# q and k of a fused attention and mixer kernel: turned on the tensor engine with PSUM evictions, or turned in 32x32 blocks on VectorE and placed by DMAs inside SBUF

## The chip, the cores and the metric

The kernel runs on one core of one Trainium2 chip. The metric is the device time of one execution in microseconds (us). Most executions of one kernel agree within about 1%, so differences of a few per cent are read from several executions. PE is the tensor engine (PEld its weight loads), DVE is VectorE, ACT is ScalarE, POOL is GpSimd, and SP is SyncE, which here only issues DMAs. "Clock" is the share of full speed that the chip granted to the tensor engine.

## The reference, cut to what matters

```python
# q, k, v: (8 batches, 8 heads, 576, 64), s: (8, 8, 576)
scores = scale * q @ k.T
cum = cumsum(max(s, 0))
scores = where(causal, -1e9, scores + min(-(cum[:, None] - cum[None, :]), 0))
attn = softmax(scores) @ v                      # per batch and head
x = attn.transpose(0, 2, 1, 3).reshape(8, 576, 512)
u = x + (x.T @ U @ V).T                         # mixing over the sequence, U: (576, 32)
out = u + max(u @ w_ch1, 0) @ w_ch2             # 512 -> 2048 -> 512
```

In these kernels both operands of the score product have head_dim (64) on the partitions and the sequence along the free axis: the page before lists line 223 as `68*128 68x128`, 64 rows of head_dim and 4 of the bias. In memory they lie the other way round, so q and k of all 64 heads are turned once.

## The kernel before

It works in bf16 and goes through head pairs, four pairs to a batch. `slots` hold a pair's score operands: 64 partitions of q and k, and 4 more partitions with the rows that carry the bias. q and k are loaded with sequence row 8p + t on partition p (72 partitions). Each head takes eight PE transposes into PSUM and two copies that evict it and put the columns in order:

```python
def transposes(n):                              # n: head pair
    b, hp = divmod(n, PB)
    slot = slots[n % NSLOT]
    if b > 0:
        nc.sync.dma_start(out=slot[D:KA, :, 0 : 2 * S], in_=rows_hbm[...])
    for hh in range(2):
        h = 2 * hp + hh
        tp = pwork().bitcast(BF16)[...]
        for c, src in enumerate((q_t[b], k_t[b])):
            for t2 in range(4):
                nc.tensor.transpose(            # line 202
                    tp[:, c, t2, :], src[:, h, ds(t2 * 128, 128)], identity[:TP, :TP]
                )
        dst = slot[0:D, hh, 0 : 2 * S].rearrange("p (c m t two) -> p c m t two", c=2, t=4, two=2)
        for par in range(2):
            copy = nc.scalar.copy if n < 2 else nc.vector.tensor_copy
            copy(dst[:, :, :, :, par], tp[par * D : par * D + D].rearrange("p c t m -> p c m t"))  # 208
        yield
```

The tensor engine is kept busy by "filling". The two large products of the previous batch (`chanmix`, 32 steps a batch) are generators, and every step of the attention work is followed by one step of filling:

```python
def run(gen):
    for _ in gen:
        step_fill()
# ... the opening: batch 0 without filling ...
for n in range(PB, NP + 1):
    b, hp = divmod(n, PB)
    if hp == 0 and b + 1 < B:
        alloc_qk(b + 1)
        load_qk(b + 1, 0, H)
        load_v(b + 1)
    if n + 1 < NP:
        run(transposes(n + 1))                  # one pair ahead
    if n < NP:
        run(scores(n))                          # PE, then exp on ACT, then masks on DVE
    if n > PB:
        run(values(n - 1))                      # PE, then normalization on DVE into x_sb
        if hp == 0:
            run(seqmix(b - 1))                  # its first matmul ("mixing") reads x_sb
            fill.append(chanmix(b - 1))
```

At the end of each batch the mixing matmul waits for the last normalization, and the filling of the next batch waits for the mixing.

The softmax here doesn't subtract the row's maximum and nothing guards it: scores larger than these inputs give would overflow.

## Time and profile before

| | before |
|---|---|
| time, median of 3 | 414.27 us (412.5, 414.27, and one execution of 1405.88 that is an outlier and is counted in the median) |
| PE busy | 391.6 us of the span of 412.1 |
| DVE, ACT busy | 228.5 us, 197.8 us |
| chain of waits | 91% PE |

The head of the page: busy us of each engine, its share of the span and its instructions, then busy tenths and granted clock in 40 equal slices.

```profile
span 412.1 us, 8636 instructions
...
PE 391.6 (95%) x3624; PEld 227.0 (55%) x3624; DVE 228.5 (55%) x452; ACT 197.8 (48%) x378; POOL 55.2 (13%) x73
...
PE   6188999989999999999999999999999999999996
...
PEclk9558999989999999999999999999999999999999
DMA  7999999992531945191619071100110001001002
```

PE is full except in the first slices, at the ninth (82 to 93 us), and at the very end. DVE has room. The DMA engines are full (nines in the DMA row) from the second through the ninth slice: weights and inputs are loading.

The chain of work that ended last, in order of time (start, duration, engine and line); first where filling and transposes alternate, then the hole at the end of batch 1.

```profile
47.59 0.26 PE pwork L202 x8
47.85 0.86 PE pwork L361 x4
48.71 0.26 PE pwork L202 x8
...
84.52 0.67 DVE slot_99 L208
85.19 0.37 DVE x_sb L286
...
85.59 0.80 DVE slot_99 L208
...
90.34 2.13 PE pwork L299 x5
```

One head's eight transposes put 0.26 us on the chain. The second part shows the hole: the filling has run out, and copies of line 208 and a slow mixing (L299: 2.13 us here, 1.08 us one batch later, at 133.98 us) stand in the chain. The granted clock from 88 to 92 us was 0.64.

The costs that the change removes, in the groups of instructions (line, engine, operation, output and input, shape, count; busy us and mean ns of one; idle time before and its releaser).

```profile
L208 DVE COPY slot_97<-pwork 64x576 bf16<-64x576 bf16 x24 | 19.2, 800 | 4.5 <-PE pwork L202 4.1
...
L202 PE MATMUL pwork<-identity,q_sd 72*128 72x72 bf16 x256 | 18.7, 198 | 1.4 <-ACT slot_96 L208 1.2
```

And one batch of the steady state, in the table by stretches (stretch, length, busy us and counts of PE, PEld, DVE, ACT, POOL; then clock, DMA share, GB/s):

```profile
134.00:177.00 43.00, 43.00 (x432) 25.38 (x431) 27.84 (x54) 22.51 (x44) 5.60 (x7) 1.00 0.49 69
```

PE is busy in all 43.00 us at full clock. This part of the kernel is bound by PE.

### The profile page before, as it was taken

To read this page: it belongs to the slowest core of one execution; us is meant where nothing else is said; L and a number is where in the kernel's file an instruction comes from. 1 tells how busy PE (TensorE), PEld (TensorE's weight loads), DVE (VectorE), ACT (ScalarE), POOL (GpSimd) and SP (SyncE) were. 2 spreads that over 40 slices of the span, in tenths; PEclk is the share of its full clock that TensorE was granted. 3 is DMA by queue.
4 is the path that set the end of the run, shared out by engine and by line. 5 is a ranking of instruction groups with operands and counts; after the bars stand their busy time and mean duration, and the time that the engine had idled before them with its cause. 6 is when DMAs were issued, how large, how long until landed. Compare 5 with 4: busy or idle time off the path is not lost.

```text
span 412.1 us, 8636 instructions
## 1 busy us (share of the span) xinstructions
PE 391.6 (95%) x3624; PEld 227.0 (55%) x3624; DVE 228.5 (55%) x452; ACT 197.8 (48%) x378; POOL 55.2 (13%) x73
## 2 busy tenths in 40 slices
PE   6188999989999999999999999999999999999996
PEld 2176556565556555555556556655565565444442
DVE  8267675686566756685666756575667545002011
ACT  3295384373743575337633663377336730530610
POOL 8721144040100310041004100000000000000000
PEclk9558999989999999999999999999999999999999
DMA  7999999992531945191619071100110001001002
GB/s 109 154 229 170 179 121 123 163 105 14 76 70 54 85 55 93 53 84 23 99 55 108 6 117 54 54 3 3 37 57 13 0 27 52 25 27 55 24 25 76
DMA packets 59301, 29.68 MB, mean 72 GB/s; under 512 B 42302, under 2 KB 53598, under 8 KB 59262
## 3 DMA queue, kind: packets, MB, share of 16 engines
q0 software_dynamic: 53360, 18.44, 52.4%
q1 hardware_dynamic: 5902, 10.69, 7.6%
q8 instruction: 28, 0.46, 0.5%
q14 instruction: 11, 0.09, 0.1%
HBM read 37.51 MB, written 9.95 MB: 115 GB/s over the span
## 4 chain that ended last, share of the span: by engine, by line
PE 91%; ACT 3%; DVE 2%; DMA 2%; issue 1%; ACTq 0%
PE pwork L361 30%; PE pwork L374 30%; PE pscore L223 11%; PE pwork L276 7%; PE pwork L202 4%; PE pwork L299 2%; PE pwork L385 2%; DMA slot_95<-hT 2%; PE pwork L320 2%; PE pscore L118 2%; PE pwork L312 1%; DVE uT L328 1%; DVE slot_99 L208 1%; ACT slot_96 L208 1%; ACT slot_95 L208 1%
## 5 line engine op out<-in xcount | busy, mean ns | idle before, releaser
L374 PE MATMUL pwork<-w_sb,hT 128*128 128x512 bf16 x576 | 143.8, 379 | 0.0
L361 PE MATMUL pwork<-uT,w_sb 128*128 128x512 bf16 x576 | 140.5, 379 | 0.4 <-DVE uT L328 0.4
L368 ACT ACTIVATE hT<-pwork 128x512 bf16<-128x512 f32 x144 | 87.4, 608 | 83.8 <-PE pwork L361 83.3
L361 PEld LDWEIGHTS <-w_sb 128*128 128x128 bf16 x576 | 51.1, 98 | 47.7 <-issue 0.9
L374 PEld LDWEIGHTS <-hT 128*128 128x128 bf16 x576 | 50.2, 98 | 42.7
L394 DVE COPY o_sb<-pwork 128x512 f32<-128x512 f32 x36 | 24.9, 692 | 70.8 <-PE pwork L385 70.8
L234 ACT ACTIVATE pT_89<-pscore 128x512 bf16<-128x512 f32 x32 | 19.2, 600 | 49.3 <-PE pscore L223 49.3
L234 ACT ACTIVATE pT_88<-pscore 128x512 bf16<-128x512 f32 x32 | 19.3, 604 | 42.4 <-PE pscore L223 42.4
L285 DVE RECIPROCAL rec<-pwork 128x5 f32<-128x5 f32 x64 | 12.2, 194 | 49.1 <-PE pwork L276 48.9
L286 DVE TENSOR_TENSOR x_sb<-pwork,rec 128x320 bf16<-128x320 f32 x64 | 31.0, 490 | 1.9
L235 DVE TENSOR_TENSOR pT_88<-pT_88,keep 128x512 bf16<-128x512 bf16 x32 | 13.1, 413 | 22.9 <-ACT pT_88 L234 22.9
L223 PE MATMUL pscore<-slot_95 68*128 68x128 bf16 (+4 forms) x126 | 15.6, 255 | 10.2 <-DMA slot_95<-hT 10.2
L276 PEld LDWEIGHTS <-pT_88 128*128 128x128 bf16 x480 | 20.1, 100 | 6.7 <-issue 0.2
L276 PEld LDWEIGHTS <-pT_89 128*128 128x128 bf16 x480 | 19.8, 100 | 7.1 <-issue 0.2
L243 ACT ACTIVATE pT_88<-pscore 128x512 bf16<-128x512 f32 x32 | 19.6, 612 | 7.5 <-PE pscore L223 6.2
L328 DVE CAST uT<-pwork 128x512 bf16<-128x512 f32 x32 | 20.1, 683 | 5.2 <-PE pwork L320 5.2
L202 PEld LDWEIGHTS <-q_sd 72*128 72x128 bf16 x256 | 16.1, 99 | 12.2 <-issue 1.6
L243 ACT ACTIVATE pT_89<-pscore 128x512 bf16<-128x512 f32 x32 | 19.3, 602 | 6.7 <-PE pscore L223 6.6
L208 DVE COPY slot_97<-pwork 64x576 bf16<-64x576 bf16 x24 | 19.2, 800 | 4.5 <-PE pwork L202 4.1
L208 DVE COPY slot_99<-pwork 64x576 bf16<-64x576 bf16 x24 | 19.2, 799 | 3.8 <-PE pwork L202 3.4
L208 DVE COPY slot_96<-pwork 64x576 bf16<-64x576 bf16 x24 | 19.2, 800 | 2.3 <-PE pwork L202 2.0
L202 PE MATMUL pwork<-identity,q_sd 72*128 72x72 bf16 x256 | 18.7, 198 | 1.4 <-ACT slot_96 L208 1.2
(91 smaller groups left out, 454.9 us busy)
## 6 DMA issues: line engine op xcount, KB each, us to landing
out_dram<-o_sb SPq DMA_DIRECT2D x36, 256.0 KB
w_sb<-in_moe_w_ch_dram POOLq DMA_DIRECT2D x2, 2048.0 KB, 25.1
q_sd<-in_q_dram POOLq DMA_DIRECT2D x7, 576.0 KB, 8.1
k_sd<-in_k_dram POOLq DMA_DIRECT2D x7, 576.0 KB, 11.2
v_slot_121<-in_v_dram POOLq DMA_DIRECT2D x12, 128.0 KB, 7.4
v_slot_124<-in_v_dram POOLq DMA_DIRECT2D x12, 128.0 KB, 5.3
v_slot_127<-in_v_dram POOLq DMA_DIRECT2D x8, 128.0 KB, 10.8
rows_hbm<-hT SPq DMA_DIRECT2D x1, 504.0 KB
```

What stands on the lines that cost most here:

```text
L202: nc.tensor.transpose(tp[:, c, t2, :], src[:, h, ds(t2 * 128, 128)], identity[:TP, :TP])
L208: copy(dst[:, :, :, :, par], tp[par * D : par * D + D].rearrange("p c t m -> p c m t"),)
L223: nc.tensor.matmul(dst, lhsT=kT[:, ds(j * 128, 128)], rhs=qT[:, lo:hi], start=True, stop=True,)
L234: nc.scalar.activation(pT[:, hh, 0:512], diag, EXP, scale=scale)
L243: nc.scalar.activation(pT[:, hh, 512:1024], far, EXP, scale=scale)
L276: nc.tensor.matmul(po[:, i, :], lhsT=pT[:, hh, ds(place(j, i), 128)], rhs=vt[:, j, h, :], start=(j == 0), stop=(j == i), skip_group_check= ...
L286: nc.vector.tensor_tensor(x_sb[:, :, ds(h * D, D)], po[:, :, 0:D], rec.to_broadcast([128, 5, D]), op=ALU.mult,)
L328: nc.vector.tensor_copy(uT[:, dt, ds(b * S, 512)], ut)
L361: nc.tensor.matmul(f1, lhsT=w1_sb[:, kt, ds(nf * 128, 128)], rhs=uT[:, kt, ds(g * 512, 512)], start=(kt == 0), stop=(kt == 3),)
L368: nc.scalar.activation(hT[:, nf, :], f1, RELU)
L374: nc.tensor.matmul(f2, lhsT=hT[:, nf, ds(i * 128, 128)], rhs=w2_sb[:, nf, :], start=(nf == 0), stop=False, skip_group_check=True,)
L394: nc.vector.tensor_copy(o_sb, f2)
```

## The change

The intent: take the transposes off PE for all batches but the first. The change uses DVE's `transpose` (STREAM_TRANSPOSE in the traces) and lays its operands out for it as 32x32 blocks. q and k of four heads are loaded on 128 partitions, 32 per head, with sequence row 18p + t of a head on its partition p. One DVE transpose turns q of four heads, another turns k, into `turned`; then eight DMAs from SBUF to SBUF place the blocks on partitions 0 to 63 of the slot. A group of four heads is placed two pairs ahead. Line 232 of the new kernel is the DVE transpose, line 238 the placing DMAs.

```diff
+    def load_qk(b):
+        for g in range(2 * b, 2 * b + 2):
+            qk_t[g] = loads.tile([128, 2, ST * D], BF16, tag="qk_sd", name="qk_sd", bufs=4)
+            for c, src in enumerate((q, k)):
+                nc.gpsimd.dma_start(
+                    out=qk_t[g][:, c, :],
+                    in_=src[b, ds(4 * (g % 2), 4)].rearrange("h (p t) d -> (h p) (t d)", p=32),
+                )
 ...
+    def place(g):
+        slot = slots[g % NSLOT]
+        nc.sync.dma_start(out=slot[D:KA, :, 0 : 2 * S], in_=rows_hbm[...])
+        src = qk_t.pop(g)
+        turned = work.tile([128, 2, 2, S], BF16, tag="turned", name="turned")
+        for c in range(2):
+            nc.vector.transpose(
+                turned[:, c].rearrange("p e (m t) -> p e t m", t=ST),
+                src[:, c].rearrange("p (t e d) -> p e t d", t=ST, e=2),
+            )
+        for a in range(4):
+            for e in range(2):
+                nc.sync.dma_start(
+                    out=slot[ds(32 * e, 32), a, 0 : 2 * S].rearrange("p (c s) -> p c s", c=2),
+                    in_=turned[ds(32 * a, 32), :, e, :],
+                )
 ...  (slots hold four heads; batch 0 keeps the PE transposes)
     for n in range(PB, NP + 1):
 ...
-        if n + 1 < NP:
-            run(transposes(n + 1))
+        if hp % 2 == 0 and n + 2 < NP:
+            place(n // 2 + 1)
```

`ST` is 18. The output order `(m t)` with t = 18 means that two values which follow one another in a transpose's output pattern land 18 bf16, that is 36 bytes, apart. That puts the sequence in its natural order, so that the DMAs can move runs of 1152 bytes.

More of the change, by code (lines that the diff above doesn't have):

```diff
@@ L44 @@
     TP, TT = 72, 8
+    ST = S // 32
     NG = B * S // 512
@@ L66, with load_first @@
     nc.sync.dma_start(out=s_sb, in_=s.rearrange("b h s -> (b h) s"))
-    q_t, k_t = {}, {}
-    def alloc_qk(b):
-        q_t[b] = loads.tile([TP, H, TT * D], BF16, tag="q_sd", name="q_sd")
-        k_t[b] = loads.tile([TP, H, TT * D], BF16, tag="k_sd", name="k_sd")
-    def load_qk(b, h, n):
-        for dst, src in ((q_t[b], q), (k_t[b], k)):
+    qk_early = work.tile([128, NF, 512], BF16, tag="hT", name="hT").rearrange(
+        "p a b -> p (a b)"
+    )
+    q_0, k_0 = (
+        qk_early[:TP, ts(c, H * TT * D)].rearrange("p (h t) -> p h t", h=H) for c in range(2)
+    )
+    def load_first(h, n):
+        for dst, src in ((q_0, q), (k_0, k)):
             nc.gpsimd.dma_start(
                 out=dst[:, ds(h, n), :],
-                in_=src[b, ds(h, n)].rearrange("h (p t) d -> p h (t d)", p=TP),
+                in_=src[0, ds(h, n)].rearrange("h (p t) d -> p h (t d)", p=TP),
             )
-    alloc_qk(0)
-    load_qk(0, 0, 2)
+    qk_t = {}
+    def load_qk(b):
[6 more added lines that the diff above has]
+                )
+    load_first(0, 2)
     identity = consts.tile([128, 128], BF16)
     make_identity(nc, identity)
-    load_qk(0, 2, 2)
-    load_qk(0, 4, 4)
+    load_first(2, 2)
+    load_first(4, 4)
     keep = consts.tile([128, 4, 128], BF16)
@@ L107 @@
         nc.vector.memset(pT[:, :, 1600:], 1.0)
-    NSLOT = 5
+    NSLOT = 3
     SK = 5 * 128
-    slots = [consts.tile([128, 2, S + SK], BF16, name=f"slot{i}") for i in range(NSLOT)]
+    slots = [consts.tile([128, 4, S + SK], BF16, name=f"slot{i}") for i in range(NSLOT)]
     for slot in slots:
@@ L137 @@
             nc.sync.dma_start(
-                out=slots[n][D:KA, hh, 0 : 2 * S],
+                out=slots[n // 2][D:KA, 2 * (n % 2) + hh, 0 : 2 * S],
                 in_=rows[2 * n + hh : 2 * n + hh + 1].rearrange("n r c s -> n r (c s)"),
@@ L177 @@
     nc.gpsimd.dma_start(out=w1_sb, in_=moe_w_ch1.rearrange("(kt kp) n -> kp kt n", kp=128))
-    alloc_qk(1)
-    load_qk(1, 0, H)
+    load_qk(1)
     nc.gpsimd.dma_start(out=w2_sb, in_=moe_w_ch2.rearrange("(kt kp) n -> kp kt n", kp=128))
@@ L184, with head_of, first_transposes @@
     x_of = {}
-    def transposes(n):
-        b, hp = divmod(n, PB)
-        slot = slots[n % NSLOT]
-        if b > 0:
-            nc.sync.dma_start(
-                out=slot[D:KA, :, 0 : 2 * S],
-                in_=rows_hbm[:, ds(2 * n, 2)].rearrange("r n c s -> r n (c s)"),
-            )
+    def head_of(n, hh):
+        return slots[(n // 2) % NSLOT][:, 2 * (n % 2) + hh, :]
+    def first_transposes(n):
         for hh in range(2):
-            h = 2 * hp + hh
+            h = 2 * n + hh
             tp = pwork().bitcast(BF16)[:, : 2 * 4 * TP].rearrange(
@@ L199, in transposes @@
             )
-            for c, src in enumerate((q_t[b], k_t[b])):
+            for c, src in enumerate((q_0, k_0)):
                 for t2 in range(4):
@@ L204, in transposes @@
                     )
-            dst = slot[0:D, hh, 0 : 2 * S].rearrange("p (c m t two) -> p c m t two", c=2, t=4, two=2)
+            dst = head_of(n, hh)[0:D, 0 : 2 * S].rearrange(
+                "p (c m t two) -> p c m t two", c=2, t=4, two=2
+            )
             for par in range(2):
@@ L212, in transposes @@
             yield
+    def place(g):
+        slot = slots[g % NSLOT]
+        nc.sync.dma_start(
+            out=slot[D:KA, :, 0 : 2 * S],
+            in_=rows_hbm[:, ds(4 * g, 4)].rearrange("r n c s -> r n (c s)"),
+        )
+        src = qk_t.pop(g)
[4 more added lines that the diff above has]
+                src[:, c].rearrange("p (t e d) -> p e t d", t=ST, e=2),
+            )
+        for a in range(4):
+            for e in range(2):
+                nc.sync.dma_start(
+                    out=slot[ds(32 * e, 32), a, 0 : 2 * S].rearrange("p (c s) -> p c s", c=2),
+                    in_=turned[ds(32 * a, 32), :, e, :],
+                )
     def scores(n):
-        slot = slots[n % NSLOT]
         pT = pTs[n % 2]
@@ L218, in scores @@
         for hh in range(2):
-            qT = slot[0:KA, hh, 0:S]
-            kT = slot[0:KA, hh, S:]
+            qT = head_of(n, hh)[0:KA, 0:S]
+            kT = head_of(n, hh)[0:KA, S:]
             def mm(dst, j, lo, hi):
@@ L258, in scores, with spot @@
             yield
-    def place(j, i):
+    def spot(j, i):
         if i == j:
@@ L277, in values @@
                         po[:, i, :],
-                        lhsT=pT[:, hh, ds(place(j, i), 128)],
+                        lhsT=pT[:, hh, ds(spot(j, i), 128)],
                         rhs=vt[:, j, h, :],
@@ L421 @@
     for n in range(PB):
-        for _ in transposes(n):
+        for _ in first_transposes(n):
             spin(1)
@@ L427 @@
             drain(values(n - 1))
+    place(2)
     drain(values(PB - 1))
@@ L431 @@
     fill_with(4)
-    run(transposes(PB))
     for n in range(PB, NP + 1):
@@ L435 @@
         if hp == 0 and b + 1 < B:
-            alloc_qk(b + 1)
-            load_qk(b + 1, 0, H)
+            load_qk(b + 1)
             load_v(b + 1)
-        if n + 1 < NP:
-            run(transposes(n + 1))
+        if hp % 2 == 0 and n + 2 < NP:
+            place(n // 2 + 1)
         if n < NP:
```

## The prediction

> **What bounds the kernel now.** The tensor engine. The page gives PE 95% busy, VectorE (DVE) 55%, ScalarE (ACT) 48%. The chain of waits is 91% PE, 2% DMA. The table by stretches shows PE busy in all of 43.00 us from 134 to 177 us (one batch), at granted clock 1.00, with DVE busy 27.8 and ACT 22.5.
>
> **What the change removes.** From batch 1 on, 56 heads lose 8 PE transposes each and two PSUM evictions each. In the chain of waits one head's eight transposes (line 202) advance the chain by 0.26 us, so 56 x 0.26 = 14.5 us leave PE, all where PE is the chain. On DVE 112 copies of 0.80 us go (89.6 us), off the chain except at the end of batch 1.
>
> **What it adds.** Per four heads, two DVE transposes of 1152 elements per partition. [...] DVE should fall from 228 to about 177 us. Also 8 DMAs inside SBUF per four heads, each 32 partitions x 2 runs of 1152 B, 590 KB a group, 8.3 MB in all. SyncE issues took 0.24 to 0.36 us, so about 2.4 us of issue per group; landing I estimate at 2 to 8 us (the opening's row DMAs took 7.7 us under load). Each group is placed two head pairs ahead, 14 us or more after the change, so this is hidden, perhaps not for the first.
>
> **What it moves.** The filling. Chanmix has 32 steps; before, a batch offers 38 places (8 of them in transposes), so the filling of batch 1 ran out: the chain from 82.9 to 95.6 us shows DVE copies (line 208), ACT and cold matmuls (granted clock 0.64 between 88 and 92 us). It holds some 8 us of PE work, so about 4.5 us are lost. With 30 places the filling lasts; I expect about 3 us back.
>
> **What it costs.** In the opening two DVE transposes (2.7 us) come before or beside the last normalizations of batch 0 (38.75 to 39.9 us), on which the first mixing matmul waits (40.02 us); and the first placed group must land before the first scores of batch 1 (52 us before, now some 4 us earlier). Estimate +1.5 us, at worst 5. ACT comes nearer to PE in up-projection stretches (12 activations at 0.49 us start to start plus 0.3 = 6.2 of about 7.2 us per pair): +1 us in all.
>
> **Sum.** 414.3 - 14.5 - 3 + 1.5 + 1 = 399 us; range 394 to 407. Chances: faster by over 2% 0.87, within 2% 0.10, slower 0.03.
>
> **What will show each step.** Right: 64 PE transposes (batch 0 only) in place of 512; batch stretches of about 41.1 us instead of 43.2 with PE still full; DVE transposes near 1.4 us; no idle PE and clock 1.00 between 75 and 92 us; PE waiting on no DMA after 55 us. Wrong: scores of batch 1 waiting on the placing DMAs; DVE transposes of 2.5 us or more (strided 2-byte writes); PE idle waiting for ACT in pairs; batch stretches still 43 us.
>
> **What would make it wrong.** The placing DMAs queue behind the weight loads, which keep the DMA engines full until about 80 us, and stall batch 1 for several us, with a cold clock after it; or matmuls run into PSUM buffers that ACT has not emptied.

The sum came to 399 us (414.3 - 14.5 - 3 + 1.5 + 1), and all its terms still stand. One sentence is cut under "What it adds": the author's estimate of the duration of one DVE transpose, whose grounds no trace or run of this case shows. The 177 us of DVE, the 2.7 us for two transposes and the "near 1.4 us" rest on it, and so does part of the +1.5. For transposes with dense writes these were measured afterwards: 178.8 us of DVE and 2.63 us for two (`e_dense_out`), 1.37 us for one (`m_forms`). The 2 to 8 us of landing are an estimate. Its upper end is near the 7.7 us named there; near its lower end, the profile before has SP's wait of 2.6 us at line 142 for the row DMAs of line 137.

## The result, and the profile after

| | before | after |
|---|---|---|
| time, median | 412.97 us (3 runs) | 492.81 us (491.04 to 494.54, 4 runs) |
| ratio | | 1.1915, 95% interval 1.1871 to 1.196 |
| span, clock of the profiled run | 412.1 us, 0.967 | 491.8 us, 0.885 |
| PE busy / not busy | 391.6 / 20.5 us | 400.2 / 91.6 us |
| DVE busy | 228.5 us | 278.9 us |

Ratios here are taken from runs of the same rounds, so they are not quite the ratios of the medians shown. Executions over 1.5% slower than the fastest of the same kernel are left out of the means. The change is 19% slower. Nearly all of it is PE standing idle: 71 us more idle time, and its busy time, which should have fallen by 14.5 us, rose by 8.6 us, although 448 transposes had gone. The granted clock, 0.885 over the run, fits that: after the wait of 7.11 us shown below it is 0.50 from 177 to 180 us, 0.74 from 180 to 183, and 1.00 again from 183 to 200.

The head of the page after:

```profile
PE 400.2 (81%) x3176; PEld 220.9 (45%) x3176; DVE 278.9 (57%) x366; ACT 195.4 (40%) x378; POOL 58.9 (12%) x87
...
PE   5391395886597869695995869699999999999996
...
PEclk9556588798698979888897979999999999999999
```

The holes recur until the twenty-sixth slice, which ends at 320 us, and then stop. The last transpose starts at 312.1 us and ends at about 317. Before it PE is never full for long; after it PE is full, at full clock (busy for all 160.00 us from 320 to 480 us, at 1.00).

The chain and the group, from the same page after:

```profile
PE 57%; DVE 32%; DMA 5%; ACT 2%; issue 2%; SPq 1%; DVEq 0%; ACTq 0%
...
L232 DVE STREAM_TRANSPOSE turned<-qk_sd 128x1152 bf16<-128x1152 bf16 x28 | 142.1, 5138 | 2.7 <-DMA slot<-turned 2.7
```

DVE went from 2% to 32% of the chain. One transpose takes 5138 ns where the prediction had about 1.4 us; 28 of them take 142.1 us, against the 38.0 us that `e_dense_out` below shows for dense writes.

The same 43 us in the table by stretches, after:

```profile
134.00:177.00 43.00, 32.25 (x279) 17.89 (x278) 29.98 (x37) 19.73 (x40) 2.04 (x4) 0.90 0.29 60
```

PE is idle for 10.75 us of it. Note that DVE is busy in only 29.98 of 43 us, hardly more than the 27.84 before: the share of busy time does not show the trouble. What shows it is who waits for whom (waits: engine and line, releaser; total us, times, longest):

```profile
PE pwork L327 <- DVE x_sb L314: 29.7, 4, 11.1
...
PE pwork L389 <- DVE x_sb L314: 26.0, 5, 7.0
```

Line 327 is the mixing matmul, line 389 the filling. Both wait for the normalization on DVE. In the groups before, the same mixing matmul (line 299 there) had 1.2 us of idle time ahead of it. The timeline of DVE shows why the normalization is late (start, duration, line, operation; records overlap a little):

```profile
165.21 5.13 DVE L232 STREAM_TRANSPOSE turned<-qk_sd 128x1152 bf16<-128x1152 bf16 x1
169.96 0.63 DVE L263 TENSOR_TENSOR pT<-pT,keep 128x512 bf16<-128x512 bf16 x1
170.49 0.23 DVE L283 TENSOR_TENSOR pT<-pT,keep 128x128 bf16<-128x128 bf16 x1
170.62 5.11 DVE L232 STREAM_TRANSPOSE turned<-qk_sd 128x1152 bf16<-128x1152 bf16 x1
175.35 0.39 DVE L313 RECIPROCAL rec<-pwork 128x5 f32<-128x5 f32 x1
175.79 0.49 DVE L314 TENSOR_TENSOR x_sb<-pwork,rec 128x320 bf16<-128x320 f32 x1
```

In this timeline DVE runs its instructions one after the other. PE had finished its last matmul before 169.9 us and next ran at 176.96 us, after 7.11 us of waiting: most of that is one transpose of 5.11 us standing ahead of four short instructions. At the end of batch 0 it is worse, where two transposes stand ahead of the last normalization and the mixing waits 11.1 us. There the program itself puts them ahead: `place` for batch 1's first group is called before the last pair's values.

There is a second thing in this trace. In the program text, batch 1's second group of four heads is turned after the mixing of batch 0, whose DVE parts are lines 335 and 356. The timeline of DVE shows it ahead of them:

```profile
49.13 0.67 DVE L314 TENSOR_TENSOR x_sb<-pwork,rec 128x320 bf16<-128x320 f32 x1
49.73 10.00 DVE L232 STREAM_TRANSPOSE turned<-qk_sd 128x1152 bf16<-128x1152 bf16 x2
59.36 0.88 DVE L335 CAST ux<-pwork 128x512 bf16<-128x512 f32 x1
60.94 2.61 DVE L356 CAST uT<-pwork 128x512 bf16<-128x512 f32 x4 [0.70 <-PE pwork L348]
```

So the built kernel doesn't keep the program's order here: these two transposes ran from 49.73 us on, ahead of the cast at 59.36 us that precedes them in the program, and PE waited 7.0 us for line 335. So the order of issue became an object of the experiments, too.

The placing DMAs, by line (minimum, median and maximum ns of one issue on SP):

```profile
L238 SPq DMA_DIRECT2D slot<-turned x112: 585/594/859, 49.5 to 350.0; - x112
```

Eight of these make 4.7 us of issue time per group. The prediction had 2.4. It took the 0.24 to 0.36 us of the issues of lines 191 (bias rows) and 395 (output) in the profile before; the same profile also holds eight DMAs from SBUF to SBUF (line 137), at 0.57 to 0.74 us for one issue.

### The profile page after: what moved, and what is told of

Its sections match the earlier page's. It is cut to its first block, busy times and chain, and to the rows that moved or that the text cites. A ratio compares the mean times of both kernels' runs of the same rounds, so it can differ in the third digit from the quotient of the medians.

```text
span 491.8 us, 7872 instructions
## 1 busy us (share of the span) xinstructions
PE 400.2 (81%) x3176; PEld 220.9 (45%) x3176; DVE 278.9 (57%) x366; ACT 195.4 (40%) x378; POOL 58.9 (12%) x87
## 4 chain that ended last, share of the span: by engine, by line
PE 57%; DVE 32%; DMA 5%; ACT 2%; issue 2%; SPq 1%; DVEq 0%; ACTq 0%
DVE turned L232 27%; PE pwork L402 20%; PE pwork L389 19%; PE pscore L251 5%; PE pwork L304 4%; DMA slot<-turned 3%; PE pwork L327 2%; DVE x_sb L314 2%; DMA slot<-hT 2%; PE pwork L413 1%; PE pscore L130 1%; DVE slot L217 1%; ACT slot L217 1%; PE pwork L340 1%; PE pwork L348 1%
## 5 line engine op out<-in xcount | busy, mean ns | idle before, releaser
L389 PE MATMUL pwork<-uT,w_sb 128*128 128x512 bf16 x576 | 152.8, 400 | 26.0 <-DVE x_sb L314 26.0
L232 DVE STREAM_TRANSPOSE turned<-qk_sd 128x1152 bf16<-128x1152 bf16 x28 | 142.1, 5138 | 2.7 <-DMA slot<-turned 2.7
L262 ACT ACTIVATE pT<-pscore 128x512 bf16<-128x512 f32 x64 | 38.7, 605 | 147.2 <-PE pscore L251 147.1
L251 PE MATMUL pscore<-slot 68*128 68x128 bf16 (+4 forms) x576 | 73.5, 259 | 9.9 <-DMA slot<-hT 9.9
L251 PEld LDWEIGHTS <-slot 68*128 68x128 bf16 x576 | 47.4, 106 | 43.8 <-issue 17.5
L263 DVE TENSOR_TENSOR pT<-pT,keep 128x512 bf16<-128x512 bf16 x64 | 29.0, 457 | 57.4 <-ACT pT L262 57.4
L271 ACT ACTIVATE pT<-pscore 128x512 bf16<-128x512 f32 x64 | 39.2, 612 | 19.8 <-PE pscore L251 18.2
L304 PEld LDWEIGHTS <-pT 128*128 128x128 bf16 x960 | 39.9, 101 | 14.3 <-issue 1.4
L304 PE MATMUL pwork<-v_slot,pT 128*128 128x65 bf16 x960 | 42.9, 198 | 0.2
L275 ACT ACTIVATE pT<-pscore 128x512 bf16<-128x512 f32 x64 | 39.4, 616 | 0.4 <-PE pscore L251 0.3
L169 POOL DMA_DIRECT2D v_slot<-in_v_dram x32 | 28.3, 896 | 86.8 <-PE pwork L304 73.0
L327 PE MATMUL pwork<-x_sb,U_sb 128*128 128x512 bf16 x40 | 14.2, 503 | 29.7 <-DVE x_sb L314 29.7
L356 DVE CAST uT<-pwork 128x512 bf16<-128x512 f32 x32 | 21.8, 693 | 14.7 <-PE pwork L348 14.7
```

Of the source, the lines that this page charges most:

```text
L169: nc.gpsimd.dma_start(out=vt[:, t, :, 0:D], in_=v[b, :, ds(t * 128, 128), :].rearrange("h p d -> p h d"),)
L232: nc.vector.transpose(turned[:, c].rearrange("p e (m t) -> p e t m", t=ST), src[:, c].rearrange("p (t e d) -> p e t d", t=ST, e=2),)
L251: nc.tensor.matmul(dst, lhsT=kT[:, ds(j * 128, 128)], rhs=qT[:, lo:hi], start=True, stop=True,)
L262: nc.scalar.activation(pT[:, hh, 0:512], diag, EXP, scale=scale)
L263: nc.vector.tensor_tensor(pT[:, hh, 0:512], pT[:, hh, 0:512], keep.rearrange("p a b -> p (a b)"), op=ALU.min)
L271: nc.scalar.activation(pT[:, hh, 512:1024], far, EXP, scale=scale)
```

## The experiments

Theory W (writes): the transposes are slow because each value is written 36 bytes from the one before it, and PE waits behind them. Rivals: the 32x32 transpose of this size is slow in itself; the stepped reading is slow; the placing DMAs or the loads are the bottleneck; and theory Q (queue): whatever their length, the transposes are issued at a bad place in DVE's queue, ahead of work that PE needs. Eleven kernels were run.

The comparison with the reference called every run right, also the two kinds that are wrong. q and k are drawn times 0.1, so their products are tiny against the bias, and a wrong order of q and k doesn't show in the output. The comparison therefore doesn't test the placing. For the layout of the last variants the index arithmetic was replayed separately on random numbers, and it agreed; that replay is not on record. A second one, of the change and of the layout of `e_step2`, agreed as well.

### m_forms: the instruction by itself

Appended to the end of the kernel before: transposes and copies, most of 1152 elements per partition, that differ in the step between consecutive writes or in the order of reading. Nothing reads their result.

```diff
+    def stepped(tile_, T):
+        return tile_.rearrange("p (g m t) -> p g t m", m=32, t=T)
+    def blocks(ap, T):
+        return ap.rearrange("p (g t d) -> p g t d", d=32, t=T)
+    for _ in range(2):
+        nc.vector.transpose(stepped(scratch, 1), blocks(flat, 1))
+        nc.vector.transpose(stepped(scratch, 2), blocks(flat, 2))
+        # ... 3, 4, 6, 9, 12, 18; other reading orders; half the size; plain copies
```

> The kernel before, with 12 forms of the 32x32 VectorE transpose and 4 plain copies added at its end, on data that nothing reads afterwards, each twice; only their durations count, the time of the whole means nothing. All transposes but two have 1152 bf16 elements per partition; what differs is the step between successive written elements: 1, 2, 3, 4, 6, 9, 12, 18 elements (18 is the step of the changed kernel, where one took 5.12 us). Theory W (the write step is what costs): step 1 takes about 1.4 us, step 18 about 5.1 us[...]. [...] Rival I (inherent to the 32x32 transpose of this size and type): all steps take about 5.1 us. Rival R (the order of the reads): the two forms that read in the changed kernel's order (64 elements apart) take 5 us whatever they write. The half-size forms (576 elements) at step 18 and 1 separate a fixed cost from a cost per element. The plain copies tell whether a stepped write is slow without a transpose: under a theory that only the transpose is hit, the copy at step 18 stays under 1.5 us.

Measured (one look, 469.82 us, state unknown; the time of the whole means nothing here). One line each, with minimum, median and maximum ns; in order: transposes with write steps 1, 2, 3, 4, 6, 9 and 18; the changed kernel's reading order with dense writes; a plain copy with write step 18; and a dense copy.

```profile
L462 DVE STREAM_TRANSPOSE slot<-w_sb x2: 1362/1370/1378, 306.1 to 357.1; 128x1152 bf16<-128x1152 bf16 x2
L463 DVE STREAM_TRANSPOSE slot<-w_sb x2: 1450/1454/1458, 308.5 to 358.9; 128x1152 bf16<-128x1152 bf16 x2
L464 DVE STREAM_TRANSPOSE slot<-w_sb x2: 2069/2086/2104, 310.0 to 360.5; 128x1152 bf16<-128x1152 bf16 x2
L465 DVE STREAM_TRANSPOSE slot<-w_sb x2: 2699/2720/2740, 312.2 to 362.9; 128x1152 bf16<-128x1152 bf16 x2
L466 DVE STREAM_TRANSPOSE slot<-w_sb x2: 3985/3991/3997, 316.5 to 366.1; 128x1152 bf16<-128x1152 bf16 x2
L467 DVE STREAM_TRANSPOSE slot<-w_sb x2: 5192/5200/5207, 321.4 to 370.4; 128x1152 bf16<-128x1152 bf16 x2
L469 DVE STREAM_TRANSPOSE slot<-w_sb x2: 5047/5074/5100, 337.7 to 381.7; 128x1152 bf16<-128x1152 bf16 x2
L473 DVE STREAM_TRANSPOSE slot<-w_sb x2: 1320/1332/1344, 348.3 to 393.4; 128x1152 bf16<-128x1152 bf16 x2
L479 DVE COPY slot<-w_sb x2: 2629/2633/2637, 289.9 to 296.3; 128x1152 bf16<-128x1152 bf16 x2
L482 DVE COPY slot<-w_sb x2: 459/460/460, 295.8 to 301.2; 128x1152 bf16<-128x1152 bf16 x2
```

With dense writes the transpose takes 1.37 us, near the 1.4 us of the prediction; so it isn't slow in itself. The changed kernel's reading order with dense writes takes 1.33 us, and with step 18 it takes 5.05; so the transpose's reading isn't the cause. Write step 18 alone brings 5.07 us. Theory W holds for the instruction. It is not the transpose alone that suffers: the plain copy goes from 0.46 to 2.63 us (and to 1.19 when it only reads with step 18). Half the elements take about half the time (2.64 us at step 18, 0.76 dense), so most of the cost goes with the elements.

Between dense writes and step 18 the time rises with the step and then stops: 1.45 us at step 2, 2.09 at 3, 2.72 at 4, 3.99 at 6, 5.20 at 9, 5.25 at 12 (not in the block above) and 5.07 at 18. From step 2 to step 6 the times lie on a straight line, 0.18 us + 0.635 us per element of step (my fit to these four: 1.45, 2.09, 2.72, 3.99 us); from 9 to 18 they no longer rise. Steps 5, 7 and 8 were not run, and why the time stops rising is not shown.

### e_dense_out and e_copy: the slow writes taken away

`e_dense_out` writes the blocks densely. The sequence is then out of order in the slots; it is wrong.

```diff
-                turned[:, c].rearrange("p e (m t) -> p e t m", t=ST),
+                turned[:, c].rearrange("p e (t m) -> p e t m", t=ST),
```

> The changed kernel with one part undone: the transposes write their blocks one after the other (step 1) in place of 18 elements apart. Wrong result on purpose (q and k columns are out of order); every DMA, every instruction count and the filling stay. Theory W: a transpose takes about 1.4 us in place of 5.1, VectorE falls from 279 to about 175 us, PE is full again from 90 us on, and the time comes to 396 to 405 us, that is what was predicted blind. Rival I: transposes stay at 5.1 us and the time at 490. Rival P (the placing DMAs, or the lost places of filling, are what costs): transposes become short but the time stays above 460.

Measured: 418.08 us (4 runs, 416.63 to 419.38), ratio to before 1.0094 (1.0058 to 1.0131). Of the 79 us that the change had lost, 75 came back with this one line. But it is still 0.9% slower than before, not at the 396 to 405 us expected of it. In the group of transposes and in the waits:

```profile
L232 DVE STREAM_TRANSPOSE turned<-qk_sd 128x1152 bf16<-128x1152 bf16 x28 | 38.0, 1367 | 21.9 <-DMA slot<-turned 21.8
```

```profile
DVE turned L232 <- DMA slot<-turned: 21.8, 5, 8.1
```

The transposes now take 38.0 us in all, and DVE 178.8 us, about the 177 us predicted. But DVE stood still for 21.8 us, up to 8.1 us at a time, with a transpose at the head of its queue whose `turned` buffer (there are two) had not yet been read by the placing DMAs. In its timeline other work stood behind: when the longest wait (8.05 us) ended with a transpose at 79.96 us, ten more DVE instructions ran up to 85.57 us with no wait listed between them. So something of theory Q may be real as well.

`e_copy` goes further and replaces the transposes by dense copies (wrong):

```diff
-            nc.vector.transpose(
-                turned[:, c].rearrange("p e (m t) -> p e t m", t=ST),
+            nc.vector.tensor_copy(
+                turned[:, c].rearrange("p e (t m) -> p e t m", t=ST),
```

> As e_dense_out, but a plain copy of the same elements in place of each transpose (wrong result on purpose): VectorE's part of the change made as cheap as it can be, DMAs and filling untouched. Theory W: copies under 1 us, about 395 to 403 us in all, within 5 us of e_dense_out. Rival P: still above 460 us.

Measured: 411.12 us (one look, state unknown). DVE fell to 153.6 us, and yet the run missed the expected 395 to 403 us: DVE waited 28.0 us for the placing DMAs. So an instruction of a third of the dense transpose's length (453 against 1367 ns) did not make the change fast. That points to the place of the instruction rather than its length; the next runs test it.

### e_pieces: the same slow writes, cut short

Each transpose is cut into six of 192 elements per partition, with the same write step, and these are handed out two at a time between the other steps; each is held behind one of DVE's instructions shortly before it in the program (`last[0]`). The first two groups still run nearly in one go. The result is right. The core of the edit:

```diff
+            for e in range(2):
+                for t in range(0, ST, 6):
+                    with tc.issue_after(last[0].ins):
+                        nc.vector.transpose(
+                            turned[:, c, e].rearrange("p (m t) -> p t m", t=ST)[:, ds(t, 6), :],
+                            src[:, c].rearrange("p (t e d) -> p e t d", t=ST, e=2)[:, e, ds(t, 6), :],
+                        )
+                    yield
```

> The changed kernel, right result, with the full cost of the stepped writes kept but each transpose cut into 6 pieces (192 elements, about 0.85 us at the same cost per element) that are held, two at a time, between VectorE's other work of the next pair of heads; the first two groups are still nearly in one go. VectorE's busy time stays near 280 us or rises a little. It separates two readings of the loss under theory W. If the loss comes from the length of one uninterrupted stretch (5 to 10 us, in which softmax masks, normalizations and evictions wait in line), the time falls to 415 to 435 us. If VectorE's total busy time in the attention part is what binds (some 35 of the 41 us of a batch), it stays above 465 us.

Measured: 453.15 us (4 runs, 452.24 to 456.7), ratio 1.0957 (1.091 to 1.1004). It lies between the ranges of the two theories. The group of pieces, and what PE's mixing matmul (line 332 here) waited for:

```profile
L236 DVE STREAM_TRANSPOSE turned<-qk_sd 128x192 bf16<-128x192 bf16 x168 | 148.1, 1101 | 0.0
```

```profile
PE pwork L332 <- DVE x_sb L319: 32.0, 7, 11.1
```

The pieces take 148.1 us in all, so DVE does as much as in the change. As they are also held in place, the fairer comparison is `e_after_pin` below (478 us): about 25 us come from cutting the long instructions and spreading them between other work, which this run doesn't separate, and 40 us over before remain. The mixing still waited 32.0 us for normalizations, in seven waits; the longest, 11.1 us, is at the first group, which was not spread. That suggests that the amount of slow DVE work costs time too, not only the length of one instruction; how the 40 us divide was not taken apart further.

### e_dense_pin: dense writes and the transposes held in program order

> As e_dense_out (418 us, wrong result on purpose), and every VectorE transpose is held in its program place; before, the build's scheduler moved them ahead. In e_dense_out VectorE stood still 21.8 us in five waits of transposes for a buffer that the placing DMAs had not yet released, and PE behind it. Theory Q (transposes issued too early stop VectorE's in-order queue while placing DMAs land slowly under the loads): these waits fall under 5 us, and the time falls by 5 to 12 us, to 406 to 413. Rival (the stall is the DMA landing itself, on which the scores wait): waits move from VectorE to PE's scores, the time stays within 3 us of 418.

```diff
-            nc.vector.transpose(
-                turned[:, c].rearrange("p e (m t) -> p e t m", t=ST),
+            tc.keep_in_program_order(nc.vector.transpose(
+                turned[:, c].rearrange("p e (t m) -> p e t m", t=ST),
                 src[:, c].rearrange("p (t e d) -> p e t d", t=ST, e=2),
-            )
+            ))
```

Measured (wrong like `e_dense_out`): 402.65 us (6 runs, 399.09 to 404.82), ratio 0.9714 (0.9679 to 0.975), better than expected. The group now shows no idle time before it at all:

```profile
L232 DVE STREAM_TRANSPOSE turned<-qk_sd 128x1152 bf16<-128x1152 bf16 x28 | 36.8, 1352 | 0.0
```

The only edit against `e_dense_out` is the hold on the transposes, and it is worth 15 us: batch 2's first group is turned at 71.4 us, where `e_dense_out` turned it from 60.9 us on, and DVE's waits for the placing DMAs go from 21.8 us to none. So the second cause is shown. And as the loads and the placing DMAs are still all there, the rival that they are the bottleneck of the change falls.

### e_after_pin: the change, only held in program order

> The changed kernel with the slow stepped writes kept (18 elements apart) and only the transposes held in program place; right result. It splits the loss between the two causes that e_dense_out and e_dense_pin left: if the slow writes alone explain the loss and the order matters only beside short transposes (15 us there), the time stays between 465 and 487 us. If most of the loss was the early issue of the transposes, it falls under 440 us.

The edit is `keep_in_program_order` around the unchanged transpose. Measured: 478.04 us (4 runs, 475.07 to 478.91), ratio 1.1549 (1.1511 to 1.1587). In the timeline of DVE the casts of the mixing now come first, and the second group after them, as in the program.

```profile
53.30 0.69 DVE L335 CAST ux<-pwork 128x512 bf16<-128x512 f32 x1 [2.48 <-PE pwork L327]
54.80 2.61 DVE L356 CAST uT<-pwork 128x512 bf16<-128x512 f32 x4 [0.80 <-PE pwork L348]
...
57.65 10.06 DVE L232 STREAM_TRANSPOSE turned<-qk_sd 128x1152 bf16<-128x1152 bf16 x2
```

In these traces the hold keeps a transpose from going ahead of what precedes it in the program, but what follows it can still pass. Three of the last pair's four normalizing instructions, which follow the first group in the program, ran before it here, and the fourth still waited behind its two transposes, so that PE's mixing again waited 11.1 us.

In the table by stretches PE is busy for 197.31 of the 240 us from 100 to 340 us, at clock 0.91; in the change for 190.32, at 0.89. Holding the order alone recovers 15 us, and the slow writes keep the other 64 us over before. The two effects add up: from the change at 492.8 us, order alone gives 15 us, dense writes alone 75 us, and both give 90 us (402.65).

### e_step2 and e_step2_pin: fast writes and a right result

`m_forms` says that write step 2 is nearly free (1.45 us against 1.37 dense). So the rows are loaded as 9 runs of 2 consecutive rows per partition, and each transpose writes pairs. There are then four transposes of 576 elements per group instead of two of 1152, and each head has a load DMA of its own. The result is right.

```diff
+                for h in range(4):
+                    nc.gpsimd.dma_start(
+                        out=qk_t[g][ds(32 * h, 32), c, :].rearrange("p (r x) -> p r x", r=9),
+                        in_=src[b, 4 * (g % 2) + h].rearrange("(r p t) d -> p r (t d)", p=32, t=2),
+                    )
 ...
+            for e in range(2):
+                nc.vector.transpose(
+                    turned[:, c, e].rearrange("p (r m t) -> p r t m", r=9, t=2),
+                    src[:, c].rearrange("p (r t e d) -> p e r t d", r=9, t=2, e=2)[:, e],
+                )
```

> The changed kernel with a right result and only the layout of the loads changed: each partition gets 9 runs of 2 sequence rows instead of one run of 18, so that a transpose writes 2 elements (4 bytes) apart; four transposes of 576 elements per group in place of two of 1152, and one load DMA per head. Theory W: about 0.8 us each (m_forms: 1.45 us for 1152 at step 2), some 3.2 us per group in place of 10.2, and a time near e_dense_out: 413 to 424 us. Rival: shorter runs in the loads (256 B written each, in place of 2304) make the loads late, and the time is above 430 us.

Measured: 405.97 us (4 runs, 403.51 to 406.84), ratio 0.9802 (0.9766 to 0.9839): faster than before, but whether by 2% is unclear. It is better than expected: its transposes waited only 2.1 us for the placing DMAs, where those of `e_dense_out` waited 21.8. The builder chose another order for this form. Why it did is not settled.

`e_step2_pin` is the same with the transposes held as in `e_dense_pin`.

> e_step2 with the transposes held in their program place; right result. Theory Q: as far below e_step2 as e_dense_pin is below e_dense_out, 404 to 415 us.

Measured: 402.16 us (4 runs, 401.74 to 402.45), ratio 0.9719 (0.9691 to 0.9747). The transposes take 772 ns each (median), DVE 181.8 us in all. The hold is worth 3.8 us here and not the 15 of `e_dense_pin` that the expectation carried over: in the opening the builder had already put the transposes of `e_step2` in the same order. The finer loads have a price that doesn't show in the time: POOL, which issues them, is busy for 110.9 us against 58.9 in the change. This is the change as it was meant: right, 2.8% faster than before, and inside the predicted 394 to 407 us. Left over are waits of PE for the placing DMAs, 5.7 us in three places: 3.84 us at the first group and the rest at the second, while the opening loads fill the DMA engines (nines in the DMA row of its page from 10 to 140 us).

### v_late, v_early, v_late_early: the first groups

The remaining loss was around 45 to 100 us, where the DMA engines are full of loads (the same nines). `v_late` leaves batch 1 on PE transposes as well and starts the DVE path with batch 2. `v_early` keeps the DVE path from batch 1, and from batch 2 on places each group three pairs ahead instead of two. `v_late_early` does both, with all groups but its first placed three pairs ahead.

```diff
 # v_late, against e_step2_pin (the loads of batch 1 as before, by pairs)
-    place(2)
+    run(first_transposes(PB))
 ...
-        if hp % 2 == 0 and n + 2 < NP:
+        if n + 1 < 2 * PB:
+            run(first_transposes(n + 1))
+        if hp % 2 == 0 and n + 2 < NP and n // 2 + 1 >= PB:
             place(n // 2 + 1)
 # v_late_early, against v_late
-        if hp % 2 == 0 and n + 2 < NP and n // 2 + 1 >= PB:
-            place(n // 2 + 1)
+        if n == PB + 2:
+            place(4)
+        if n % 2 == 1 and n + 3 < NP and (n + 3) // 2 > PB:
+            place((n + 3) // 2)
```

> A version meant to beat both, right result: batch 1 still goes through PE as in the kernel before (16 us of opening DMA pressure kept away from the placing DMAs), and from batch 2 on VectorE turns with writes 2 elements apart, held in program place. 48 heads lose 0.26 us of PE each, 12.5 us. If the opening is what still costs e_dense_pin its gain, this comes to 400 to 405 us; if something in the steady batches costs it, it stays above 408 us.

Measured: 401.67 us (6 runs, 400.09 to 403.96), ratio 0.9708 (0.9676 to 0.9741); not different from `e_step2_pin`. The hole of the opening had only moved. The chain of `v_late` near 90 us:

```profile
78.90 5.30 DMA v_slot<-in_v_dram
...
84.29 2.85 DVE turned L253 x4
...
87.17 7.83 DMA slot<-turned
```

The wait of PE that belongs to it, and the stretch from 84 to 104 us:

```profile
PE pscore L272 <- DMA slot<-turned: 4.3, 1, 4.3
```

```profile
84.00:104.00 20.00, 14.79 (x131) 8.74 (x130) 9.75 (x23) 8.51 (x19) 12.92 (x20) 0.83 1.54 147
```

This is the second group turned on DVE (the first was turned at 70.9 us, and PE didn't wait for it). Its placing lands 7.83 us after its last transpose. Of these, the eight issues on SP take most: they run from 86.48 to 92.25 us, and the landing is at 95.0. Issuing them from two queues was not tried.

> e_step2_pin (402.2 us) with each group from the fourth of the new path on placed three pairs of heads ahead in place of two; right result. The placing DMAs of a group took some 8 us from their first issue to landing while the loads still ran, and PE waited 5.7 us in three places for them. If the lead is what is short there, 397 to 401 us; if the wait only sits at the first group (whose lead does not change), within 1.5 us of 402.2.

Measured: 403.72 us (6 runs, 401.63 to 404.36), ratio 0.9748 (0.9719 to 0.9777). More lead from batch 2 on gains nothing, as PE waits only at the first two groups, whose lead this edit leaves alone: 3.9 us for the first one's placing, and 2.1 us for the bias rows of the second. (Batch 2's first group is the third of the new path, not the fourth.)

> v_late (401.7 us) with every group but the first placed three pairs ahead; right result. In v_late PE stood still about 5 us near 90 us, where the second placed group landed at 95 us: with its placing some 8 us earlier this gap should close: 395 to 399 us. If it does not close, the loads of that group are late, not its placing, and the time stays above 400 us.

Measured: 396.74 us (5 runs, 395.98 to 397.22), ratio 0.9594 (0.9572 to 0.9616), the fastest of all, and right. Its page and the stretch near 90 us:

```profile
PE   6089899999999999999999999999999999999996
```

```profile
84.00:104.00 20.00, 19.57 (x204) 12.02 (x205) 12.91 (x32) 15.07 (x31) 12.86 (x21) 1.00 1.70 175
```

In the same 20 us `v_late` had PE busy for 14.79 us at clock 0.83, and the kernel before 18.46 us at 0.91. The second group is now turned at 78.4 us, 5.9 us earlier. No wait of PE for a placing DMA is left in the list. From mixing matmul to mixing matmul one batch takes about 39.0 us (159.82 to 198.77), where before it took 43.27 us. Of these 4.3 us, eight heads at 0.26 us give 2.1. About 1.7 more are, by my estimate, two steps of filling (0.86 us each) that no longer find a place in the batch and run at the end instead; the trace counts 60 of the filling's first matmuls in a batch, where before it counted 64. Each of the two edits alone gave nothing over `e_step2_pin`; together they gave some 5 us. More `turned` buffers, another way to loosen the waits, were not tried.

## Why the prediction was wrong

The prediction was 399.0 us with a range up to 407; the change took 492.8 us. Point by point:

1. "What bounds the kernel now" was right: PE, full at full clock.
2. **The step that failed is the duration of one DVE transpose, "DVE transposes near 1.4 us".** It measured 5.14 us each, 142.1 us in all. The author's estimate came out near the duration with dense writes and left out where the values are written. The instruction with dense writes does take 1.37 us (`m_forms`), so the term was right for another access pattern. The prediction even named "DVE transposes of 2.5 us or more (strided 2-byte writes)" as a sign of being wrong, but did not price it: it was in the diff, as the `(m t)` order with t = 18. Dense writes alone gave back 75 us.
3. The mechanism by which this became lost time was foreseen only for the opening ("two DVE transposes (2.7 us) come before or beside the last normalizations of batch 0"), and was missing for the other batches. DVE was only 57% busy over the run. But a DVE instruction of 5.11 us held up the four short ones behind it, among them the normalization that PE waited 7.11 us for, and PE then also ran at a lower clock (0.885 over the run). Cutting the instructions and spreading them gave about 25 us with the amount of work unchanged (`e_pieces` against `e_after_pin`).
4. "Each group is placed two head pairs ahead ... so this is hidden" failed in a way that was not foreseen. In `e_dense_out` it was less PE that waited for the placing DMAs (4.7 us) than DVE (21.8 us), for `turned` buffers that they still held, because the builder issued the transposes earlier than the program did. In the change itself this wait is short (2.7 us), why was not tested; there the early place shows as PE waiting behind the transposes. Keeping the order was worth 15 us (`e_dense_out` against `e_dense_pin`, and the change against `e_after_pin`).
5. The issue cost of the placing DMAs was mis-sized: 0.59 us each, 4.7 us per group, against 2.4. In `v_late` the second group's placing took 7.8 us from its last transpose to landing, at the upper end of the 2 to 8 us. "Perhaps not for the first" was right: in `e_step2_pin` PE waited 3.84 us for the first group.
6. Much of the rest held once the writes were mended. DVE with dense writes is 178.8 us (predicted 177). ACT didn't become the bound (in `v_late_early` it is 49% busy, PE 94%). A batch of `v_late_early` is 4.3 us shorter, which leaves room for the 2.1 us of eight heads at 0.26; that gain wasn't measured by itself. The sum, 399 us, lies near the measured time of `e_step2_pin`, 402.2 us, and with the opening mended 396.7 us. That is no test of its single terms: the 3 us that the longer filling should give back were not measured by themselves either, and the opening below shows a term that was too small.

The opening cost more than the estimated 1.5 us in `e_step2_pin`: PE is short of full there in the third to seventh slices of the page, and some 5 us lie between it and `v_late_early`, in which the later start and the longer lead work together.

## What to carry to other kernels

Price an instruction with the access pattern that it has in the kernel: a write step of 18 bf16 elements made a VectorE transpose of 1152 elements per partition 3.7 times as long as dense writes did (5.07 against 1.37 us, `m_forms`), and a different split of the rows at load time (step 2, 1.45 us) made it nearly free. An engine that is far from full can still stop the one that is: here DVE, 57% busy, kept PE waiting 7.11 us, most of it one transpose of 5.11 us. So ask how long the longest instruction in its queue is and what stands behind it. And after moving work to another engine, look in the trace at where it is really issued, and hold it in its place if it came forward; that was worth 15 us here.
